# A three-stage attention and mixture-of-experts kernel: another engine repeats the block means of v in the first attention batch, and the search constants are made in five parts

## The chip, the cores and the metric

The kernel runs on one core of one Trainium2 chip. The metric is the device time of one execution in microseconds (us). The five engines of a core that appear below are TensorE (PE, with its weight loads PEld), VectorE (DVE), ScalarE (ACT), GpSimd (POOL) and SyncE (SP), which only issues DMAs here. Each engine works through its own list of instructions in order. An instruction whose data are not ready holds up everything behind it on its engine.

## The reference, cut to what matters

```python
# 1. attention: B=4, H=8, S=768, D=64; blocks of 32, window 16
k_sum = k.reshape(B, H, 24, 32, D).max(axis=3)
v_sum = v.reshape(B, H, 24, 32, D).mean(axis=3)          # the block means of v
scores = [window scores with |i-j| < 16, else -1e9]  ++  [q . k_sum / 8 + log 32]
a   = softmax(scores)
x   = a @ concat([v, v_sum])                              # -> [3072, 512]
# 2. MoE with capacity: each token goes to one of 8 experts, greedy by gate logit, 384 per expert
x[mask_e] = relu(x[mask_e] @ w1[e]) @ w2[e]
# 3. soft MoE: 32 slots, softmax over tokens (dispatch) and over slots (combine)
out = combine @ (relu((dispatch.T @ x) @ m2w1) @ m2w2)
```

Everything is computed in float32. Products that need it are made in split precision: a rounded high part and a low part, which is the difference between the value and its high part (`wh` and `wl` for w1, two halves of `x` for the tokens).

## The kernel before

**Attention.** The 32 (batch, head) pairs are worked in 16 units of two heads; unit n belongs to batch b = n // 4 and has p = n % 4. A batch's values lie in one tile, `vw[128, 12, 8, 65]`: for each of 12 tiles T of 64 queries and each head, partitions 0 to 95 hold the 96 rows of v that the window can touch, partitions 96 to 119 hold the 24 block means of v, and column 64 holds ones (so that the product also yields the softmax sum). The block means are the same for every T, so they have to stand there twelve times. There are two such tiles, used by turns.

A unit is software-pipelined over two turns of the main loop. Turn n does, in this order of code: the transposes of k for unit n+1 (`prep_k`, L199 and L214), the score products of unit n (`score`, L268), the minimum per row (`least`, L280 and L281 on DVE), the subtraction of the minimum (`less`, L285 on POOL), the key windows of unit n+1 (`windows`, L222 on POOL), the transposes of the exponentials of unit n-1 (`trans`, L295 and L297), exponentials (L289 on ACT), block maxima of k (L231 on DVE, spread by L236 on POOL), the transposes of q (`prep_q`), then the product with the values of unit n-1 (`av`, L306), its normalisation (`norm`, L320 to L322 on DVE) and the loads of unit n+4 (`load_qk`, L111). Each of the three groups of scores of a unit has its own `least`, `less` and exponential.

In the first batch the block means are made for two heads at a time, in the turn of the unit that owns these heads: `vsum` multiplies v by a summing matrix (L177), ACT copies the sums (L185), a second small product moves them to partitions 96 to 119 (L188), ACT writes them to tile T = 0 (L189), and a DMA issued by SP copies tile 0 to tiles 1 to 11 (L190). In the later batches one `vsum` makes all eight heads, one unit ahead.

All five engines follow the order of the code (a manual schedule). SP's list therefore has the copies of L190 among the loads of k, q and v (L111, L79, L91); `load_qk(4)` and the whole of the second batch's v are issued in turn 0.

**The search constants.** The expert assignment is searched in rounds on DVE with small tables (`_assign_consts`, L464 and after): counting tables, powers, selection matrices, a triangular mask, index rows. They are made once, at the end of turn 2: some 25 small DVE instructions, the index rows by POOL (`iota`), together with the load of `phi` and its selection matrix `selr`.

**The first MoE stage** starts after the attention with products of w2 and `phi` on PE, between which the search runs (DVE tables `D_r`, `G_r`, `tie_r` and small PE products `as`). Then the tokens of the first expert are gathered (L1154 on POOL), transposed (L1169), and split into high and low parts (L1170 on ACT, L1177 on DVE). The weights of w1 come in pieces of 128 columns; `split` makes their high part on ACT (L1199) and their low part on POOL (L1200). Two pieces are split ahead of the first matmuls of L1233, the third at their start.

Of the kernel before, what the change touches and what calls it, by code (L numbers as in the profile page):

```python
# [10 lines left out]
F32 = mybir.dt.float32  # L11
# [3 lines left out]
I32 = mybir.dt.int32  # L15
# [32 lines left out]
def _attention(tc, K, ps, q, k, v, w_gate, w2, xd, L, constants, work):  # L48
# [4 lines left out]
    with ExitStack() as ctx:  # L53
# [116 lines left out]
        def vsum(b, lo, hi, pv2s):  # L170

            vw = vws[b % 2]
            n = 64 * (hi - lo)
            pv = bank([128, n], f"pv{b}_{lo}")
            for T in range(NT):
                g = T % 4
                nc.tensor.matmul(  # L177
                    pv[32 * g : 32 * g + 32, :],
                    bz[0:96, 30 - 2 * T : 62 - 2 * T],
                    vw[0:96, T, lo:hi, 0:64],  # L180
                    start=T < 4,
                    stop=T >= NT - 4,
                )
            vs = wk.tile([128, 512], F32, name=f"vs{b}_{lo}", tag="vs", bufs=1)[:, 0:n]
            nc.scalar.copy(vs, pv)  # L185
            yield
            pv2 = bank([128, n], f"pw{b}_{lo}")
            nc.tensor.matmul(pv2[96:128, :], sel, vs, start=True, stop=True)  # L188
            nc.scalar.copy(vw[96:120, 0, lo:hi, 0:64], pv2[96:120].rearrange("j (h d)->j h d", d=64))  # L189
            nc.sync.dma_start(  # L190
                vw[96:120, 1:NT, lo:hi, :], vw[96:120, 0:1, lo:hi, :].to_broadcast([24, NT - 1, hi - lo, 65])
            )

        def turned(n, src, nm_, dst, put):
# [178 lines left out]
        prep_q(0)  # L373

        VS = {}
        for n in range(NU):
            b, p = divmod(n, 4)
            if 0 < n and n + 1 < NU:
                prep_k(n + 1)
            score(n)  # L380
            if n == 0:
                prep_k(1)
            if b == 0:
                VS[p] = vsum(0, 2 * p, 2 * p + 2, None)
                next(VS[p])
            least(n, 0)
            less(n, 0)
            if n + 1 < NU:
                windows(n + 1)
            if n:  # L390
                for i in range(3):
                    trans(n - 1, i)
            exps(n, 0)
            least(n, 1)
            less(n, 1)
            if n + 1 < NU:
                summaries(n + 1)
                if p == 3 and b:
                    gate_sum(b - 1, 0)
                    gate_sum(b - 1, 1)  # L400
                prep_q(n + 1)
            if p == 2 and b:
                gate_logits(b - 1, 0)
                gate_logits(b - 1, 1)
            if b == 0:
                next(VS[p], None)
            elif p == 0:
                next(VS[b, 0], None)
            exps(n, 1)
            least(n, 2)  # L410
            if n + 1 < NU:
                summaries_out(n + 1)
            less(n, 2)
            if n:
                av(n - 1)
                norm(n - 1, 0)
                norm(n - 1, 1)
            load_qk(n + 4)
            if n > 1:
                for i in range(2):  # L420
                    gate_turn(n - 2, i)
            exps(n, 2)
            if p == 0 and b + 1 < B:
                load_ends(b + 1)
                load_v(b + 1, range(H))
            if p == 0 and b:
                store(b - 1)
            if p == 3 and b + 1 < B:
                VS[b + 1, 0] = vsum(b + 1, 0, H, None)
                next(VS[b + 1, 0])  # L430
            if n == 2:
                constants(wk)
            if n == NU - 3:
                next(work)
        n = NU - 1
# [25 lines left out]
        next(work)  # L461


def _assign_consts(tc, cp, wk, ident):  # L464
    nc = tc.nc
    C = {}
    tmp = wk.tile([128, 480], I32, name="as_tmp", tag="X", bufs=6)
    it = tmp[:, 0:64]
    nc.gpsimd.iota(it, pattern=[[1, 64]], base=0, channel_multiplier=0)
# [4 lines left out]
    for n in (32, 64):  # L474

        C["o", n] = cp.tile([128, 128], BF16, name=f"as_o{n}")
        nc.vector.memset(C["o", n], float(STEP * n // 128))
    w8i = tmp[:, 64:72]
    nc.gpsimd.iota(w8i, pattern=[[-1, 8]], base=8, channel_multiplier=0)
    C["w8"] = cp.tile([128, 8], F32, name="as_w8")  # L480
# [7 lines left out]
    nc.vector.tensor_copy(C["w23"][0:1], w8i[0:1])  # L488
    C["ones"] = cp.tile([128, 128], BF16, name="as_on")
    nc.vector.memset(C["ones"], 1.0)  # L490
    for n in (32, 64):

        J = 128 // n
        C["pick", n] = cp.tile([128, J, J, n], F16, name=f"as_pk{n}")
        for j in range(J):
            nc.vector.tensor_copy(C["pick", n][:, j], ident[:, None, j:128:J].to_broadcast([128, J, n]))
    C["tri"] = cp.tile([128, 128], BF16, name="as_tri")
    nc.vector.memset(C["tri"], 1.0)
    nc.gpsimd.affine_select(
# [21 lines left out]
    for i in range(2):  # L521
        R = cp.tile([128, 2, 26], F16, name=f"as_R{i}")
        nc.vector.tensor_scalar(R[:, :, 25:26], pi[:, None, :].to_broadcast([128, 2, 1]), 0.5, None, ALU.mult)
        C["R"].append(R)
    return C


def _assign_rounds(tc, C, wk, ps, L, ids, eis, found, placed):
# [372 lines left out]
def tile_kernel(  # L901
# [60 lines left out]
    eis = cp.tile([128, E], I32, name="eis")  # L962

    def constants(wk):
        K["C"] = _assign_consts(tc, pqp, wk, ident)
        phis = K["phis"] = pqp.tile([128, 4, NSLOT], F32, name="phis")
        nc.sync.dma_start(phis, phi.rearrange("(c p) s->p c s", p=128))

# [167 lines left out]
    with ExitStack() as c2:  # L1136
# [54 lines left out]
        def split(k):  # L1191

            fetch(k)
            while len(W) <= k and len(W) < len(RAW):
# [2 lines left out]
                wh = ring.tile([128, 4, 128], F32R, name=f"wh{r}_{u}", tag="wh", bufs=NWHL)  # L1197
                wl = ring.tile([128, 4, 128], F32R, name=f"wl{r}_{u}", tag="wl", bufs=NWHL)
                nc.scalar.copy(wh, raw)  # L1199
                nc.gpsimd.tensor_tensor(wl, raw, wh.bitcast(F32), ALU.subtract)  # L1200
                W[8 * r + u] = (wh, wl)

        def fetch_p(r):
# [537 lines left out]
```

## Time and profile before

| what | value |
|---|---|
| median of 3 runs | 593.9 us (591.81, 593.9, 593.99) |
| the profiled execution's own time | 592.53 us |
| its span in the trace | 590.8 us |
| busy: PE, DVE, ACT, POOL | 538.5, 344.0, 315.3, 216.1 us |
| mean granted clock of TensorE | 0.976 |

The profiled execution's time is 1.7 us longer than its span, and it lies within the three runs. PE is busy for 91% of the span. The first four fortieths of the span (59 us) are the exception: there PE is busy for 5, 7, 6 and 7 tenths, and from the fifth on for 8 or 9 tenths and more. The chain of waits that ends last is PE for 60%, DVE for 21%, ACT and DMA for 4% each.

In the rows below a time in us at the start of a row is its start from the beginning of the span. In rows of the timeline a bracket at the end says how long the engine stood idle before the row, and what released it.

### The profile page before, as it was taken

The page shows a single profiled execution, that of the slowest core. Times are in us where ns is not written, and L with a number is a line of the kernel's source. Part 1 is how long each engine was busy: PE and PEld are TensorE (multiplying, and loading weights), DVE is VectorE, ACT ScalarE, POOL GpSimd, SP SyncE. Part 2 cuts the span into 40 slices and gives each one's busy share as a digit, 9 for nine tenths or more (in the row PEclk, how much of TensorE's full clock was granted, in tenths as well). Part 3 has the DMA queues.
Part 4 walks back from the last instruction along what each step waited for, and adds up shares of the span by engine and source line. Part 5 has one row for each costly group of instructions (what it writes and reads, how often), then busy time and mean ns, then how long its engine had stood idle before and what let it go on. Part 6 is the DMA issues. An engine that isn't in the chain of part 4 may idle for free.

```text
span 590.8 us, 15076 instructions
## 1 busy us (share of the span) xinstructions
PE 538.5 (91%) x5765; PEld 393.4 (67%) x5765; DVE 344.0 (58%) x1113; ACT 315.3 (53%) x670; POOL 216.1 (37%) x262
## 2 busy tenths in 40 slices
PE   5767999999999999889999998999999999979994
PEld 3556677777787766477766676767677867753474
DVE  5655887887872766688777798855232213031342
ACT  2743787887865667354635536544664535321231
POOL 3531563544530000425244473445446463321000
PEclk9986999999999999899999999999999999998997
DMA  9996299698974897436358484674949896779997
GB/s 192 203 195 132 66 243 226 160 223 182 299 275 149 291 383 224 116 100 196 100 163 281 131 265 153 215 235 152 303 156 302 287 327 209 264 246 372 354 302 208
DMA packets 158898, 131.17 MB, mean 222 GB/s; under 512 B 43380, under 2 KB 130068, under 8 KB 158828
## 3 DMA queue, kind: packets, MB, share of 16 engines
q1 hardware_dynamic: 153020, 115.81, 68.9%
q0 software_dynamic: 4368, 13.37, 7.0%
q10 hardware_dynamic: 1440, 1.05, 0.6%
q8 instruction: 45, 0.74, 0.5%
q14 instruction: 25, 0.20, 0.1%
HBM read 113.98 MB, written 14.02 MB: 217 GB/s over the span
## 4 chain that ended last, share of the span: by engine, by line
PE 60%; DVE 21%; ACT 4%; DMA 4%; issue 3%; SPq 2%; POOL 2%; another core or an unknown queue 1%; POOLq 0%; DVEq 0%; ACTq 0%
PE ph L1233 15%; PE pwt L1032 4%; PE pp L997 3%; PE pS L268 3%; DMA w<-in_moe_w_dram 3%; PE po L306 3%; PE po L1692 3%; PE mh L1629 3%; DVE G_r L745 3%; PE pt L1254 2%; PE pS L1412 2%; PE l L1274 2%; PE pA L1307 2%; SPq L91 2%; PE pf L1651 2%
## 5 line engine op out<-in xcount | busy, mean ns | idle before, releaser
L1233 PE MATMUL ph<-x,wh 128*128 128x384 f32 x512 | 145.3, 359 | 0.0
L1200 POOL TENSOR_TENSOR wl<-raw,wh 128x512 fp32r<-128x512 f32 x64 | 85.1, 1333 | 132.0 <-ACT wh L1199 119.4
L1233 PEld LDWEIGHTS ph<-x,wh 128*128 128x128 f32 x512 | 88.4, 189 | 22.1 <-issue 19.4
L1233 PE MATMUL ph<-x,wl 128*128 128x384 f32 x256 | 88.4, 345 | 0.0
L285 POOL TENSOR_TENSOR X<-X,mn 128x480 f32<-128x480 f32 x48 | 47.3, 985 | 69.9 <-DVE mn L281 42.2
L1244 ACT ACTIVATE hT<-ph 128x384 f32<-128x384 f32 x64 | 31.2, 488 | 74.7 <-PE ph L1233 63.4
L1233 PEld LDWEIGHTS ph<-x,wl 128*128 128x128 f32 x256 | 48.1, 188 | 0.0
L1154 POOL DMA_INDIRECT xg<-xd,ids x24 | 23.3, 972 | 61.6 <-PE pwt L1032 52.4
L306 PE MATMUL po<-vw,AT 120*64 120x65 f32 x768 | 30.3, 235 | 13.3 <-DMA vw<-vw 13.3
L280 DVE TENSOR_TENSOR X<-pS,nm 128x480 f32<-128x480 f32 x48 | 31.4, 655 | 18.6 <-PE pS L268 17.9
L306 PEld LDWEIGHTS po<-vw,AT 120*64 120x64 f32 x768 | 27.3, 147 | 20.1 <-DMA vw<-vw 14.0
L1199 ACT CAST wh<-raw 128x512 fp32r<-128x512 f32 x64 | 39.9, 623 | 0.0
L1047 ACT COPY wt<-pwt 128x512 f32<-128x512 f32 x60 | 33.1, 590 | 11.8 <-PE pwt L1032 9.8
L214 ACT COPY kT<-pk 64x384 f32<-64x384 f32 x62 | 31.2, 503 | 12.1 <-PE pk L199 11.3
L1032 PE MATMUL pwt<-ident,pw 128*128 128x128 f32 x224 | 33.6, 281 | 1.1 <-ACT wt L1047 0.6
L1254 PE MATMUL pt<-ident,hT 128*128 128x128 f32 x192 | 33.9, 277 | 0.0
L281 DVE TENSOR_REDUCE mn<-X 128x4 f32<-128x480 f32 x48 | 31.4, 653 | 4.1
L268 PE MATMUL pS<-kwin,qT 64*64 64x120 f32 x768 | 32.1, 276 | 1.8 <-POOL kwin L236 1.8
L1256 ACT COPY h<-pt 128x384 f32<-128x384 f32 x64 | 30.2, 474 | 5.8 <-PE pt L1254 5.6
L289 ACT ACTIVATE X<-X 128x480 f32<-128x480 f32 x48 | 29.3, 610 | 6.5 <-POOL X L285 5.9
L268 PEld LDWEIGHTS pS<-kwin,qT 64*64 64x64 f32 x768 | 28.1, 138 | 5.2 <-POOL kwin L236 2.4
L1290 POOL DMA_INDIRECT cd<-ce,ids x24 | 24.5, 1020 | 17.6 <-DVE den L1404 13.7
(291 smaller groups left out, 1066.0 us busy)
## 6 DMA issues: line engine op xcount, KB each, us to landing
mw<-in_moe_w_dram SPq DMA_DIRECT2D x55, 512.0 KB
raw<-in_moe_w_dram SPq DMA_DIRECT2D x64, 256.0 KB
w<-in_moe_w_dram SPq DMA_DIRECT2D x30, 512.0 KB
pw<-in_moe_w_dram SPq DMA_DIRECT2D x28, 512.0 KB
vw<-in_v_dram SPq DMA_DIRECT2D x32, 240.0 KB
kt<-in_k_dram SPq DMA_DIRECT2D x32, 192.0 KB
qt<-in_q_dram SPq DMA_DIRECT2D x32, 192.0 KB
xd<-xb POOLq DMA_DIRECT2D x4, 1536.0 KB
```

Source lines behind the costliest of these rows:

```text
L214: lambda r, d, s: nc.scalar.copy(d, s) if n or r else nc.vector.tensor_copy(d, s),
L268: nc.tensor.matmul(PS[n][i][64 * u : 64 * u + 64, j, :], qT[r, 64 * T : 64 * T + 64], kwin[r, T, :], start=True, stop=True,)
L280: nc.vector.tensor_tensor(X, PS[n][i], nm[:, i // 2], ALU.add)
L281: nc.vector.tensor_reduce(mn, X, AX.X, ALU.min)
L285: nc.gpsimd.tensor_tensor(X, X, MN.pop((n, i))[:, :, None].to_broadcast([128, 4, 120]), ALU.subtract)
L306: nc.tensor.matmul(PO[n][T // 6][64 * (T % 2) : 64 * (T % 2) + 64, T // 2 % 3, hh, :], AT[n, i][0:120, j, 64 * u : 64 * u + 64], vw[0:120, ...
L1032: nc.tensor.transpose(pt[:, dc], PW[e, q][t][:, 128 * dc : 128 * dc + 128], ident)
L1047: nc.scalar.copy(wt[:, :, 128 * t : 128 * t + 128], pt)
L1199: nc.scalar.copy(wh, raw)
L1200: nc.gpsimd.tensor_tensor(wl, raw, wh.bitcast(F32), ALU.subtract)
L1233: nc.tensor.matmul(ph, a[:, dc], b[:, dc], start=dc == n == 0, stop=(dc, n) == (3, 2),)
L1254: nc.tensor.transpose(pt[:, c], HT[r, fc][:, 128 * c : 128 * c + 128], ident)
```

## The change

Three edits:

1. In the first batch only, POOL repeats the block means: L190's DMA is replaced by a `tensor_copy` of tile 0 to tiles 1 to 11 (64 columns; the ones in column 64 are set once at the start anyway). It stands in the code behind the third `less` of the unit, and so behind it in POOL's list. Later batches keep the DMA.
2. `_assign_consts` becomes a generator in four parts, and `phi` with `selr` is the fifth. One part is made at the end of each of the turns 0 to 4, where before all came at the end of turn 2. The index rows on POOL go with their parts.
3. The low parts of the first two pieces of w1 (first expert) are made on DVE. All others stay on POOL.

The core of the diff:

```diff
@@ vsum
-            nc.sync.dma_start(
-                vw[96:120, 1:NT, lo:hi, :], vw[96:120, 0:1, lo:hi, :].to_broadcast([24, NT - 1, hi - lo, 65])
+            if b:
+                nc.sync.dma_start(
+                    vw[96:120, 1:NT, lo:hi, :], vw[96:120, 0:1, lo:hi, :].to_broadcast([24, NT - 1, hi - lo, 65])
+                )
+                return
+            yield
+            nc.gpsimd.tensor_copy(
+                vw[96:120, 1:NT, lo:hi, 0:64],
+                vw[96:120, 0:1, lo:hi, 0:64].to_broadcast([24, NT - 1, hi - lo, 64]),
             )
@@ main loop of the attention
+        steps = constants(wk)
         for n in range(NU):
...
             if b == 0:
-                next(VS[p], None)
+                next(VS[p])
...
             less(n, 2)
+            if b == 0:
+                next(VS[p], None)
...
-            if n == 2:
-                constants(wk)
+            if n < 5:
+                next(steps, None)
@@ _assign_consts: a yield behind as_o, behind as_on, behind as_pk and at the end
@@ split
-                nc.gpsimd.tensor_tensor(wl, raw, wh.bitcast(F32), ALU.subtract)
+
+                (nc.gpsimd if r or u > 1 else nc.vector).tensor_tensor(wl, raw, wh.bitcast(F32), ALU.subtract)
```

**POOL at the end of turn 0.** X0_2 is the third group of scores of unit 0, X1_0 the first of unit 1, vw0 the values of the first batch, as_tmp the index row for the first part of the constants. Before:

```order
L285 TENSOR_TENSOR X0_2_290<-X0_2_290,mn0_2_291 128x480
L285 TENSOR_TENSOR X1_0_367<-X1_0_367,mn1_0_368 128x480
L222 COPY kwin0_93<-kT0_95 128x12x96
L285 TENSOR_TENSOR X1_1_395<-X1_1_395,mn1_1_396 128x480
L236 COPY kwin0_93<-ks2_400 128x12x24
```

Now:

```order
L292 TENSOR_TENSOR X0_2_289<-X0_2_289,mn0_2_290 128x480
L196 COPY vw0_97<-vw0_97 24x11x2x64
L479 IOTA as_tmp_313 128x64
L292 TENSOR_TENSOR X1_0_377<-X1_0_377,mn1_0_378 128x480
L229 COPY kwin0_93<-kT0_95 128x12x96
```

The copy of the block means and the index row stand between the last subtraction of one unit and the first of the next.

**DVE at the same place.** Before:

```order
L280 TENSOR_TENSOR X0_2_290<-pS0_2_207,nm_149 128x480
L281 TENSOR_REDUCE mn0_2_291<-X0_2_290 128x4
L280 TENSOR_TENSOR X1_0_367<-pS1_0_325,nm_149 128x480
L281 TENSOR_REDUCE mn1_0_368<-X1_0_367 128x4
L280 TENSOR_TENSOR X1_1_395<-pS1_1_326,nm_149 128x480
```

Now:

```order
L287 TENSOR_TENSOR X0_2_289<-pS0_2_207,nm_149 128x480
L288 TENSOR_REDUCE mn0_2_290<-X0_2_289 128x4
L483 CAST as_cn32_315<-as_tmp_313 128x128
L483 CAST as_cn64_317<-as_tmp_313 128x128
L487 MEMSET as_o32_319 128x128
L487 MEMSET as_o64_321 128x128
L287 TENSOR_TENSOR X1_0_377<-pS1_0_335,nm_149 128x480
```

The first part of the constants stands ahead of the minimum of unit 1, and its first instruction reads POOL's index row. The second part does the same at the end of turn 1.

**SP in turn 0.** vw1 is the tile of the second batch, kt5 and qt5 are the loads of unit 5. Before:

```order
L162 DMA wg_167<-in_moe_w_gate_dram 128x4x8
L190 DMA vw0_97<-vw0_97 24x11x130
L111 DMA kt4_296<-in_k_dram 128x3x128 x2
L111 DMA qt4_299<-in_q_dram 128x3x128 x2
L79 DMA vw1_98<-in_v_dram 80x8x64 x2
L91 DMA vw1_98<-in_v_dram 96x10x64 x8
L190 DMA vw0_97<-vw0_97 24x11x130
L111 DMA kt5_460<-in_k_dram 128x3x128 x2
```

Now:

```order
L162 DMA wg_167<-in_moe_w_gate_dram 128x4x8
L111 DMA kt4_296<-in_k_dram 128x3x128 x2
L111 DMA qt4_299<-in_q_dram 128x3x128 x2
L79 DMA vw1_98<-in_v_dram 80x8x64 x2
L91 DMA vw1_98<-in_v_dram 96x10x64 x8
L111 DMA kt5_470<-in_k_dram 128x3x128 x2
```

The copies are gone, the order of the loads is the same.

**DVE ahead of the first expert.** M_b is a step of the search, x the low part of the first expert's tokens. Now (before, the rows of wl0 were not there and stood on POOL right ahead of that of the third piece):

```order
L767 TENSOR_SCALAR D1_r2_4071<-D_r20_4067 128x24
L894 TENSOR_TENSOR KM_b1_3647<-KM_b1_3647,KM_b0_3139 128x24
L558 TENSOR_REDUCE M_b2_4074<-L2_s2_4053 128x24
L1218 TENSOR_TENSOR wl0_0_4086<-raw0_0_3880,wh0_0_4085 128x512
L1218 TENSOR_TENSOR wl0_1_4090<-raw0_1_3891,wh0_1_4089 128x512
L1194 TENSOR_TENSOR x_3023<-px0_0_4097,x_3023 128x384
L1194 TENSOR_TENSOR x_3023<-px0_1_4108,x_3023 128x384
```

The two subtractions stand between the search and the tokens' low parts. The order of PE and of ACT is unchanged throughout.

## Rows read from the trace of the kernel before

**Rows 1.** Busy time by stretch; columns: stretch, PE, PEld, DVE, ACT, POOL, clock, DMA
```profile
40.00:60.00 20.00, 11.37 (x168) 9.91 (x170) 9.19 (x42) 6.74 (x15) 3.89 (x10) 0.74 0.76 137
```
**Rows 2.** Timeline of PE, first batch; columns: start, us, engine, line, operation, idle before
```profile
27.14 0.33 PE L306 MATMUL po<-vw,AT 120*64 120x65 f32 x2
29.74 2.63 PE L306 MATMUL po<-vw,AT 120*64 120x65 f32 x46 [2.27 <-DMA vw<-vw]
...
48.39 2.86 PE L306 MATMUL po<-vw,AT 120*64 120x65 f32 x46 [9.16 <-DMA vw<-vw]
...
59.47 1.67 PE L306 MATMUL po<-vw,AT 120*64 120x65 f32 x48
...
65.86 1.87 PE L268 MATMUL pS<-kwin,qT 64*64 64x120 f32 x48
```
**Rows 3.** Timeline of SP's queue: the second batch's v and the copy behind it
```profile
30.45 11.61 SPq L91 DMA_DIRECT2D vw<-in_v_dram  x8
42.16 1.14 SPq L190 DMA_DIRECT2D vw<-vw  x1
```
**Rows 4.** Groups of POOL up to 100 us, by form; columns: busy us, mean ns, idle
```profile
L285 POOL TENSOR_TENSOR X<-X,mn 128x480 f32<-128x480 f32 x24 | 23.7, 986 | 35.4 <-DVE mn L281 18.1 <-DVE rc L320 6.6 <-PE pA L295 4.5
L222 POOL COPY kwin<-kT 128x1152 f32<-128x1152 f32 x8 | 9.1, 1143 | 3.8 <-ACT kT L214 2.6 <-issue 1.2
L236 POOL COPY kwin<-ks 128x288 f32<-128x288 f32 x9 | 3.8, 421 | 0.6 <-DVE ks L231 0.6
...
L118 POOL MEMSET vw<- 32x512 f32 x2 | 1.0, 516 | 0.0
```
**Rows 5.** Timeline of POOL: the third subtraction of unit 0, an index row
```profile
21.20 0.99 POOL L285 TENSOR_TENSOR X<-X,mn 128x480 f32<-128x480 f32 x1 [0.90 <-DVE mn L281]
...
41.90 0.19 POOL L469 IOTA as_tmp<- 128x64 int32 x1
```
**Rows 6.** Timeline of DVE: start of unit 1, the constants, unit 3, start of unit 4
```profile
21.44 0.66 DVE L280 TENSOR_TENSOR X<-pS,nm 128x480 f32<-128x480 f32 x1 [0.32 <-PE pS L268]
...
52.19 0.35 DVE L473 CAST as_cn<-as_tmp 128x128 bf16<-128x128 int32 x2
...
53.29 0.97 DVE L496 CAST as_pk<-ident 128x128 f16<-128x128 f32 x6
54.24 0.17 DVE L498 MEMSET as_tri<- 128x128 bf16 x1
...
56.07 0.39 DVE L970 TENSOR_REDUCE selr<-ident 128x32 f32<-128x128 f32 x1
...
56.98 0.65 DVE L280 TENSOR_TENSOR X<-pS,nm 128x480 f32<-128x480 f32 x1
...
62.19 0.65 DVE L281 TENSOR_REDUCE mn<-X 128x4 f32<-128x480 f32 x1
...
64.06 0.56 DVE L322 TENSOR_TENSOR xb<-po,rc 128x384 f32<-128x384 f32 x1
66.95 0.66 DVE L280 TENSOR_TENSOR X<-pS,nm 128x480 f32<-128x480 f32 x1 [2.33 <-PE pS L268]
```
**Rows 7.** Timeline of ACT: k of unit 2, third exponential of unit 1
```profile
22.86 2.08 ACT L214 COPY kT<-pk 64x384 f32<-64x384 f32 x4
...
30.05 0.60 ACT L289 ACTIVATE X<-X 128x480 f32<-128x480 f32 x1 [0.82 <-POOL X L285]
```
**Rows 8.** Waits of PE from 110 to 250 us: total, times, longest
```profile
PE as L776 <- DVE G_r L745: 2.3, 1, 2.3
```
**Rows 9.** Timeline of POOL ahead of the first expert
```profile
239.28 3.73 POOL L1200 TENSOR_TENSOR wl<-raw,wh 128x512 fp32r<-128x512 f32 x3
```
**Rows 10.** Timeline of DVE at the same place
```profile
239.97 3.09 DVE L849 TENSOR_SCALAR tie_r<-tie_r,as 128x24 f32<-128x24 f32 x1 [1.23 <-PE pwt L1032]
...
249.49 0.25 DVE L804 SCALAR_TENSOR_TENSOR D_r<-D_r,as,E_r 128x24 bf16<-128x24 f32 x1 [1.50 <-PE as L801]
```
**Rows 11.** All instructions of L849: min/median/max ns, first and last start
```profile
L849 DVE TENSOR_SCALAR tie_r<-tie_r,as x7: 230/235/3092, 214.9 to 413.2; 128x24 f32<-128x24 f32 x7
```

More of the change, by code (lines that the diff above doesn't have):

```diff
@@ L461, in _attention, with _assign_consts @@
         next(work)
-def _assign_consts(tc, cp, wk, ident):
+def _assign_consts(tc, C, cp, wk, ident):
     nc = tc.nc
-    C = {}
     tmp = wk.tile([128, 480], I32, name="as_tmp", tag="X", bufs=6)
@@ L477, in _assign_consts @@
         nc.vector.memset(C["o", n], float(STEP * n // 128))
+    yield
+    tmp = wk.tile([128, 480], I32, name="as_tmp2", tag="X", bufs=6)
     w8i = tmp[:, 64:72]
@@ L490, in _assign_consts @@
     nc.vector.memset(C["ones"], 1.0)
+    yield
     for n in (32, 64):
@@ L496, in _assign_consts @@
             nc.vector.tensor_copy(C["pick", n][:, j], ident[:, None, j:128:J].to_broadcast([128, J, n]))
+    yield
+    tmp = wk.tile([128, 480], I32, name="as_tmp3", tag="X", bufs=6)
     C["tri"] = cp.tile([128, 128], BF16, name="as_tri")
@@ L524, in _assign_consts @@
         C["R"].append(R)
-    return C
+    yield
 def _assign_rounds(tc, C, wk, ps, L, ids, eis, found, placed):
@@ L964, in constants @@
     def constants(wk):
-        K["C"] = _assign_consts(tc, pqp, wk, ident)
+        C = K["C"] = {}
+        for _ in _assign_consts(tc, C, pqp, wk, ident):
+            yield
         phis = K["phis"] = pqp.tile([128, 4, NSLOT], F32, name="phis")
```

## Prediction

> **What bounds the kernel now.** I read the page first: PE is busy nine tenths of the time everywhere but in the first 60 us, so what is to be won without removing PE work lies there. The view by stretches says how much: from 40 to 60 us PE is busy for 11.37 us of 20, at a granted clock of 0.74 [rows 1]. The timeline of PE then names the holes. In turn 1 the products with v start, stop after two matmuls and go on when the copied block means arrive, 2.27 us later; in turn 2 the same takes 9.16 us [rows 2]. SP's queue says why the second is so long: the copy stands behind eight loads of the next batch's v, is issued at 42.16 and has arrived at 48.39, 6.2 us after [rows 3, 2]. Behind each hole PE runs slower for a while: 46 of these matmuls take 2.63 and 2.86 us, and 48 take 1.67 us later [rows 2]. DVE shows a second delay behind that hole: the constants stand between 52.19 and 56.98, and unit 3's minima only follow them [rows 6].
>
> **Edit 1, and the part of edit 2 that stands in its way.** With the DMA gone, the block means come from POOL one turn before PE wants them. What paces the first units then is a loop through DVE, POOL and ACT. I follow it with stretches that the trace shows.
>
> Lengths: the DVE work of a unit from its first X to the end of its third mn is 56.98 to 62.84, 5.86 us without a hole, its normalisation runs to 64.62, 1.8 us more [rows 6]. A subtraction on POOL is 0.99 [rows 5], an exponential 0.60 [rows 7]. From the start of the copies of k on ACT to the products with v on PE it is 22.86 to 27.14, 4.28 us [rows 7, 2]. The new copy has 11 x 2 x 64 = 1408 elements per partition. POOL copies 1152 in 1.143 us and 288 in 0.421, so 0.84 ns for each further element: 1.143 + 256 x 0.84 ns = 1.36 us [rows 4]. Only 24 partitions take part; 512 elements on 32 partitions in 0.516 us show no penalty for that [rows 4]. Bounds: 0.42, the 288-element row, and the rate of the two-input subtraction, 986 ns for 480, which gives 2.9 us [rows 4]. I take 1.36, from the two rows of the same operation.
>
> The Trainium skill (GPSIMD Engine Reference, section 3.1 on elementwise work) puts the best case at about 1.8 cycles per element, 512 elements in 768 ns: by that page 1408 elements are an estimated 2.1 us, and the forecast below would be 1.6 us later. The trace's 1152 elements in 1.143 us are faster than that rule, so the rows decide.
>
> Turn 0: POOL's third subtraction ends at 22.19 [rows 5], the copy at 23.55, the index row (0.19 [rows 5]) at 23.74. DVE meanwhile stands before its first constant, since that reads the index row. Parts one and two of the constants took 52.19 to 53.29 together [rows 6]; I give each half, 0.55. Unit 1's first X starts at 24.3 instead of 21.44 [rows 6], 2.9 us later. The cover for this is that PE and ACT still work on unit 0, so av of unit 0 keeps its 27.14, now without the stop.
>
> Turn 1: third mn of unit 1 at 24.3 + 5.86 = 30.15; subtraction, 31.15; exponential, 31.8; then ACT copies k. Av of unit 1 at 31.8 + 4.28 = 36.1, where before it went on at 48.39. POOL: copy to 32.5, index row to 32.7. DVE has normalised unit 0 by 32.0 and waits again for the index row; part two, and X of unit 2 at 33.25.
>
> Turn 2: mn at 33.25 + 5.86 = 39.1, subtraction 40.1, exponential 40.7, av of unit 2 at 45.0, against 59.47 [rows 2]: 14.5 us earlier. From there PE has no hole to speak of up to the scores of unit 4: before, 59.47 to 65.86 [rows 2]. So these come at 51.4, also 14.5 us earlier, provided DVE is there: it ends unit 2 at 39.1 + 1.8, makes part three (53.29 to 54.24, 0.95 [rows 6]) by 41.85, unit 3's third mn by 47.7 and its normalisation by 49.5. Part four waits for POOL (subtraction 48.7, copy 50.05) and took 54.24 to 56.07 [rows 6], so it ends near 51.9. Unit 4's first X came 1.09 us after the scores began (66.95 to 65.86 [rows 6, 2]), that is now 52.5: hidden, with 0.6 us to spare. Without the two waits for index rows the loop would be 2.5 us faster; that price is in the 14.5. The clock's loss goes too, as no hole of PE in this account exceeds 1 us; it is part of the difference read from PE's starts and is not added.
>
> The loads: v of the second batch is wanted near 47.5, and was all issued by 42.06 [rows 3], now 1 us sooner; with the copy's 6.2 us as delay it has arrived by 47.3. This is the tightest place of the account, and I charge nothing.
>
> **Rest of edit 2.** Part five (selr, 56.07 to 56.98, 0.9 us [rows 6]) falls into turn 4, where PE is busy and DVE is some tenths short of it: between 0 and 0.9, I take 0.4 lost.
>
> **Edit 3.** At 239.28 POOL makes three low parts in a row, 3.73 us [rows 9]. A DVE instruction that normally takes 0.235 us [rows 11] starts at 239.97, and ends when they do, at 243.06 [rows 10]: it was held by POOL. The search then reaches PE late, which waits 2.3 us, its longest wait between 110 and 250 us [rows 8]. With one low part left there, it ends at 239.28 + 1.24 = 240.5, and DVE's instruction 2.4 us earlier; PE's 2.3 us go. The two on DVE cost about 0.7 each (480 elements are 0.65 [rows 6]), 1.4, ahead of the tokens' low parts. DVE waits there for PE (1.50 us [rows 10]), so most of it is hidden. Bounds: +2.3 if all is hidden, -1.4 if the hold stays and nothing is. I take +2.0.
>
> **Sum.** 14.5 - 0.4 + 2.0 = 16.1 us off the profiled execution's 592.5: 576.4. The runs' median is 1.4 above that execution, which would make 577.8; I forecast **577**. PE is dense behind 60 us, and the loads hang on its progress, so all later work moves up with it.
>
> **Rivals.**
> - *POOL's copy is long and DVE waits for it.* A copy of c us enters the loop in turns 0 and 1, and beyond 0.6 us more in turn 3. At 2.9 us: 2 x 1.53 + 0.9 = 4.0 us later, 581. For it: the 24 partitions and the repeated source are in no row. Against: the two copy rows. Chance 0.15.
> - *The loads become the bound of the first batch.* If the queue needs some 3 to 6 us more than PE's new pace, v of the second batch or k of unit 5 is what PE waits for: 580 to 583. For it: the margin of 0.2 us. Against: PE waited for no other load there, and less is in the queue. Chance 0.10.
> - *The index rows cost DVE less than I charge*, because the copy is shorter or DVE catches up: up to 2.5 us better, 574. Chance 0.08.
> - *The change does not do what it says:* if the products of unit n-1 waited for the copy of unit n, not of n-1, PE would stand still again from 27.5 to 32.5, and each turn would grow from 9 to some 11.7 us: 585. Against: before, the products of unit 0 went on at 29.74, long before the second copy was issued. Chance 0.02.
> - *Slower than before.* The same POOL copy, if it were several times its price, would be worse than the DMA: beyond 1.36 us each microsecond counts in turns 0, 1, 3 and, beyond 1.65 us more, in turn 2. The loss is 4 x (c - 1.36) - 2.25 us; it eats the 16.1 us at c = 6.0, and at 7 us the time is 597. Nothing in the rows is near that. Chance 0.03, other mishaps included.
>
> **How the numbers follow.** The forecast has 0.62, with 574 to 580 as its own range. The range of 8 in 10 takes in the larger copy and most of the loads' rival: 572.5 to 583. About 0.5% is what a measurement of this kernel can tell from no change, 3 us. Faster by more than that is everything but the last rival and a sliver: 0.95; within it 0.02; slower 0.03.
>
> **What would show it.** Right: no wait of PE for vw in turns 1 and 2; four POOL copies of 24 partitions near 1.36 us; DVE idle for POOL's index row for some 2.5 us ahead of as_cn and under 1 us ahead of the second part; scores of unit 4 near 51.4; tie_r at about 0.6 us and PE's wait for G_r gone. Wrong: copies of 3 us and more, PE waiting for loads of v, k or q before 60 us, a clock below 1 between 30 and 60 us, or a hole of PE at the low parts on DVE; or a saving at unit 4 that is gone again at the end.

## The result, and the profile after

The changed kernel took 577.14 us (median of 4 runs, 575.30 to 580.23) where the kernel before took 593.16 in runs on the same chip (4 runs, 591.81 to 593.99): a ratio of 0.972, with a 95% interval of 0.968 to 0.976. Run again on another chip it was 572.57 against 589.84, 0.970 (0.967 to 0.973). The profiled execution took 575.3 us, with a span of 573.6.

The stretches that answer to [rows 1], with the same columns, are now filled, at the full clock:

```profile
20.00:40.00 20.00, 17.20 (x309) 13.82 (x311) 15.53 (x39) 15.35 (x31) 12.44 (x16) 1.00 1.20 195
40.00:60.00 20.00, 19.36 (x304) 14.05 (x296) 17.93 (x47) 16.24 (x32) 13.19 (x18) 1.00 0.75 164
```

PE's timeline, against [rows 2] (start, us, engine, line, operation). The products with v of units 0, 1 and 2 run in one piece, in 1.67 us each, and the scores of unit 4 start at 51.84, 14.0 us earlier than before:

```profile
27.07 1.67 PE L313 MATMUL po<-vw,AT 120*64 120x65 f32 x48
...
36.31 1.67 PE L313 MATMUL po<-vw,AT 120*64 120x65 f32 x48
...
45.92 1.67 PE L313 MATMUL po<-vw,AT 120*64 120x65 f32 x48
...
51.84 1.87 PE L275 MATMUL pS<-kwin,qT 64*64 64x120 f32 x48
```

From 20 to 250 us PE's waits for the copies of the block means fall from 13.3 us in five waits to 2.0 us in three, those of the later batches, which keep the DMA.

POOL's timeline: the new copies of units 0 to 2 (the fourth, at 49.98, is like them), and the first index row behind one of them:

```profile
22.20 1.36 POOL L196 COPY vw<-vw 24x1408 f32<-24x1408 f32 x1
23.64 0.19 POOL L479 IOTA as_tmp<- 128x64 int32 x1
...
31.42 1.36 POOL L196 COPY vw<-vw 24x1408 f32<-24x1408 f32 x1
...
40.66 1.36 POOL L196 COPY vw<-vw 24x1408 f32<-24x1408 f32 x1
```

DVE's timeline, against [rows 6]: parts one to four of the constants, each behind POOL. Three wait for an index row (the bracket is the idle time before, and what ended it). The picks of part three, as_pk, stand in no bracket, but take 1.91 us instead of 0.97: they start while POOL's copy of 40.66 runs. (The picks are the selection matrices of the search.)

```profile
23.86 0.36 DVE L483 CAST as_cn<-as_tmp 128x128 bf16<-128x128 int32 x2 [2.79 <-POOL as_tmp L479]
24.42 0.59 DVE L287 TENSOR_TENSOR X<-pS,nm 128x480 f32<-128x480 f32 x1
...
33.02 0.17 DVE L493 CAST as_w<-as_tmp 128x8 f32<-128x8 int32 x1 [1.02 <-POOL as_tmp L491]
...
41.16 1.91 DVE L509 CAST as_pk<-ident 128x128 f16<-128x128 f32 x6
...
52.15 0.36 DVE L520 CAST as_sf<-as_si 128x384 f16<-128x384 int32 x1 [1.38 <-POOL as_si L518]
...
53.01 0.65 DVE L287 TENSOR_TENSOR X<-pS,nm 128x480 f32<-128x480 f32 x1
```

The later units stay 14.0 us early up to the scores of unit 11 (115.09 against 129.13). Between these and unit 12's, 0.8 us are lost, all of it in the block sums of the fourth batch's v: 24 matmuls take 3.69 us here and took 2.87 before, at full clock in both. The timeline of their weight loads (PEld) has a wait for a DMA after the second, which before has none. The sums read only v and a constant, so the DMA that they need is a load of v, although the trace names one of q that ended with it.

```profile
122.95 0.14 PEld L177 LDWEIGHTS pv<-vw,bz 96*32 96x32 f32 x2 [0.17 <-issue]
123.84 0.19 PEld L177 LDWEIGHTS pv<-vw,bz 96*32 96x32 f32 x8 [0.75 <-DMA qt<-in_q_dram]
```

At the first gather POOL is 13.2 us early (222.40 against 235.61). Then edit 3 acts. POOL's timeline there, against [rows 9], one low part in place of three; the fourth comes 17.1 us early (before: 256.36), so 3.9 us were won between:

```profile
222.40 1.06 POOL L1171 DMA_INDIRECT xg<-xd,ids  x1 [52.45 <-PE pwt L1049]
...
226.08 1.28 POOL L1218 TENSOR_TENSOR wl<-raw,wh 128x512 fp32r<-128x512 f32 x1
239.25 1.28 POOL L1218 TENSOR_TENSOR wl<-raw,wh 128x512 fp32r<-128x512 f32 x1 [11.90 <-DVE G_r L760]
```

DVE there, against [rows 10], and PE's products of w2 and phi (pp): tie_r ends with POOL's one low part, PE no longer waits for G_r, and the two groups of pp take 1.49 and 1.50 us, where before they took 2.46 and 2.08.

```profile
226.75 0.65 DVE L864 TENSOR_SCALAR tie_r<-tie_r,as 128x24 f32<-128x24 f32 x1 [1.23 <-PE pwt L1049]
...
233.90 1.28 DVE L1218 TENSOR_TENSOR wl<-raw,wh 128x512 fp32r<-128x512 f32 x2
```
```profile
229.12 1.49 PE L1014 MATMUL pp<-wt,phis 128*32 128x256 f32 x20
230.54 0.20 PE L803 MATMUL as<-c_r,as_pk 128*128 128x8 f16 x2
230.68 1.50 PE L1014 MATMUL pp<-wt,phis 128*32 128x256 f32 x22
```

At the end of the program 17.2 us of span are left: what was won at these two places reaches the end.

### The profile page after: what moved, and what is told of

Its sections match the earlier page's. It is cut to its first block, busy times and chain, and to the rows that moved or that the text cites. A ratio compares the mean times of both kernels' runs of the same rounds, so it can differ in the third digit from the quotient of the medians.

```text
span 573.6 us, 15062 instructions
## 1 busy us (share of the span) xinstructions
PE 531.9 (93%) x5765; PEld 387.8 (68%) x5765; DVE 342.4 (60%) x1115; ACT 315.9 (55%) x670; POOL 219.0 (38%) x264
## 3 DMA queue, kind: packets, MB, share of 16 engines
HBM read 113.98 MB, written 14.02 MB: 223 GB/s over the span
## 4 chain that ended last, share of the span: by engine, by line
PE 61%; DVE 19%; DMA 6%; ACT 5%; issue 4%; POOL 3%; another core or an unknown queue 1%; SPq 0%; POOLq 0%; DVEq 0%; ACTq 0%
PE ph L1251 15%; DMA w<-in_moe_w_dram 5%; PE pwt L1049 4%; PE pp L1014 3%; PE po L1710 3%; PE pS L275 3%; PE po L313 3%; PE mh L1647 2%; PE pS L1430 2%; PE pt L1272 2%; DVE G_r L760 2%; PE l L1292 2%; PE pA L1325 2%; PE pf L1669 2%; PE pv L177 2%
## 5 line engine op out<-in xcount | busy, mean ns | idle before, releaser
L1218 POOL TENSOR_TENSOR wl<-raw,wh 128x512 fp32r<-128x512 f32 x62 | 82.6, 1334 | 132.7 <-ACT wh L1216 104.4
L313 PEld LDWEIGHTS po<-vw,AT 120*64 120x64 f32 x768 | 24.9, 137 | 8.6 <-issue 3.1
L760 DVE TENSOR_TENSOR G_r<-D_r,as_cn 128x768 bf16<-128x768 bf16 (+1 forms) x41 | 29.2, 713 | 1.2
```

The costliest lines, as they stand in the source:

```text
L313: nc.tensor.matmul(PO[n][T // 6][64 * (T % 2) : 64 * (T % 2) + 64, T // 2 % 3, hh, :], AT[n, i][0:120, j, 64 * u : 64 * u + 64], vw[0:120, ...
L760: v.tensor_tensor(G, Dg.rearrange("p (q j)->p q j", j=J)[:, :, None, :].to_broadcast([128, 24 // J, n, J]), C["cn", n][:, None].to_broadca ...
L1218: (nc.gpsimd if r or u > 1 else nc.vector).tensor_tensor(wl, raw, wh.bitcast(F32), ALU.subtract)
```

## The experiments

Kernels in one of the three groups below ran on one chip and share the runs of the kernel before.

### Each edit alone, and another queue (before: 589.72 us)

**e1_copy_only**: edit 1 alone; the constants stay in one piece in turn 2, as before. The edit in short:

```
+            yield
+            nc.gpsimd.tensor_copy(
+                vw[96:120, 1:NT, lo:hi, 0:64],
+                vw[96:120, 0:1, lo:hi, 0:64].to_broadcast([24, NT - 1, hi - lo, 64]),
+            )
```

> Edit 1 alone: POOL repeats the block means, the constants stay in one piece at the end of turn 2, the low parts stay on POOL. Theory: the DMA's place in SP's queue was the loss, and parts one and two of the constants cost the changed kernel some 2 us because DVE waits for index rows behind the copy. Then without the parts unit 1's first X is back near 21.4, the products with v of units 0 and 1 start without a wait near 27.1 and 35, and the scores of unit 4 start near 49 to 50, 2 us earlier than with edits 1 and 2 (51.84); the block of constants (4.8 us on DVE) is then partly visible in turn 3. Search and first expert as before (2.3 us wait of PE). Time about 577 to 579. Rival: the constants in one piece cost their 4.8 us in full, as they did before, and the parts are what made the gain possible; then the scores of unit 4 start at 54 or later and the time is above 581.

Measured: 581.13 us, ratio 0.986 (0.982 to 0.991). The rival was right. The products with v of unit 2 start at 43.27, 2.65 us earlier than in the kernel after, since no index row holds the first two turns; but then the undivided constants with selr stand on DVE from 39.22 until X of unit 3 follows at 43.99. PE's timeline shows what comes of it: a wait of 3.58 us, after which the six transposes of x (px) take 1.54 us (0.88 in the kernel after) and the block sums 5.14 (2.79 as a rule), and unit 4's scores come at 55.87.

```profile
43.27 1.67 PE L313 MATMUL po<-vw,AT 120*64 120x65 f32 x48
48.52 1.54 PE L349 MATMUL px<-ident,xb 128*128 128x128 f32 x6 [3.58 <-ACT vw L189]
49.99 5.14 PE L177 MATMUL pv<-vw,bz 96*32 96x512 f32 x24
...
55.87 1.87 PE L275 MATMUL pS<-kwin,qT 64*64 64x120 f32 x48
```

**e2_parts_only**: edit 2 alone; the copies stay DMAs. In the main loop:

```
-            if n == 2:
-                constants(wk)
+            if n < 5:
+                next(steps, None)
```

> Edit 2 alone: the constants in five parts, the DMA and POOL's low parts as before. Theory: the 9.2 us wait for the second copy stays (SP's order is that of before but for phi), the parts one and two vanish behind it, and only the minima of unit 3 come earlier (56.98 before, near 55 now, bounded by the scores at 53.9). Scores of unit 4 near 64, time 590 to 592, 1 to 3 us under before. Rival: the parts are worth the whole 4.8 us of the block, 588 or less.

Measured: 589.23 us, ratio 0.998 (0.996 to 1.001). PE still waits for the second copy, now for 11.40 us, and the scores of unit 4 come at 64.63, 1.2 us earlier than before. So the parts by themselves are worth about 1 us: the constants were mostly beside a hole that was there anyway.

```profile
47.66 2.86 PE L306 MATMUL po<-vw,AT 120*64 120x65 f32 x46 [11.40 <-DMA vw<-vw]
```

**e3_low_only**: edit 3 alone.

```
-                nc.gpsimd.tensor_tensor(wl, raw, wh.bitcast(F32), ALU.subtract)
+                (nc.gpsimd if r or u > 1 else nc.vector).tensor_tensor(wl, raw, wh.bitcast(F32), ALU.subtract)
```

> Edit 3 alone: two low parts on DVE. Theory: tie_r falls from 3.09 to 0.65 us, PE's wait for G_r of 2.3 us is gone, and the products of w2 and phi behind it no longer run at the lower clock, which is worth 1.5 us more; together 3.9 us between the gather of the first expert and its third low part, time near 589.5. Rival: the 3.9 us of the changed kernel come from its other alignment of search and PE; alone the edit is worth the 2.3 us of the wait less 1.3 us of DVE work, about 1 us, 592 to 593.

Measured: 585.37 us, ratio 0.994 (0.991 to 0.997). From the gather (233.67) to the fourth low part (250.52) it is 16.85 us, as in the kernel after, and 20.75 before: 3.9 us, as the theory said, with the wait for G_r gone.

**e4_act_queue**: the kernel before, with the first batch's copies issued by ACT instead of SP.

```
-            nc.sync.dma_start(
+            (nc.sync if b else nc.scalar).dma_start(
```

> The kernel before, with the first batch's copies still made by DMA but issued by ACT, right behind its own write of tile 0, not by SP. Theory: it was the place in SP's list that made the copy late; issued at 20 and 28.7 it arrives within some 6 us, before 27 and 35, so PE has no wait for it and the scores of unit 4 start at 49 to 50; time 577 to 579, like edit 1 alone. Rival: the 16 DMA engines are full with loads until 54 us, so a copy of 134 KB in small pieces is late whoever issues it; then waits of several us for the block means stay and the time is 583 or more.

Measured: 602.63 us, ratio 1.024 (1.021 to 1.027), slower. ACT's timeline (ACTq is its sequencer) shows why. ACT stood until it could issue the copy, with the exponentials behind it. In the program each DMA of SP and ACT waits for an earlier one with which it shares a counter, and the second hold ended with a load of k. So another queue didn't free the copy of the loads; it made ACT wait for them too. This run can't say what the place in SP's queue alone is worth; e9 below can.

```profile
33.72 1.41 ACTq L190 DMA_DIRECT2D vw<-vw  x1
35.18 1.10 ACT L289 ACTIVATE X<-X 128x480 f32<-128x480 f32 x2 [15.52 <-issue]
...
51.09 1.09 ACT L289 ACTIVATE X<-X 128x480 f32<-128x480 f32 x2 [8.25 <-DMA kt<-in_k_dram]
```

Alone, the edits give 8.6, 0.5 and 4.4 us, 13.4 in sum; together 17.3 (after_again, below), on a chip where the kernel before takes the same time. The 3.8 us more belong to edits 1 and 2: both together, without edit 3, give 13.8 us (e12_no_low, below), where one by one they give 9.1; edit 3 gives 0.9 us less beside them than alone. At unit 4's scores edits 1 and 2 give 14.0 us together and 10.0 and 1.2 alone, so 2.8 us of it show in the first batch; the rest is not traced to a place.

### The terms of the account (before: 594.62 us)

**e5_double**: the kernel after, with each POOL copy made twice.

```
-            nc.gpsimd.tensor_copy(
+            for _ in range(2):
+                nc.gpsimd.tensor_copy(
```

> The kernel after, with each unit's GpSimd copy of the block means made twice in a row (1.36 us more on GpSimd in each of the four turns). My step: the copy is not hidden behind GpSimd's other work, since the first subtraction of the next unit (and in turns 1 and 3 the next index row) stands behind it; so each doubling costs nearly its whole 1.36 us in three of the turns and the scores of unit 4 come 3 to 4.5 us later (near 55.5). Rival: GpSimd has slack in a unit turn, the copy costs nothing, and the scores of unit 4 stay within 1 us of 51.84.

Measured: 583.75 us, ratio 0.979 (0.973 to 0.985). The scores of units 2, 3, 4 and 5 come 1.38, 2.96, 2.84 and 3.79 us later than in the kernel after. So another 1.36 us of POOL cost 1.4 and 1.6 us in the turns 0 and 1, nothing in turn 2 and 1.0 in turn 3: the theory's three turns, 2.84 us at unit 4 where it gave 3 to 4.5, the last part a unit later. In turn 2 no index row stands behind the copy, and in the kernel after POOL is idle for 2.47 us before its next subtraction (44.49); the second copy fits in there, although the copies and the picks held each other and the pair takes 3.67 us here and 2.8 in the other turns.

```profile
43.62 3.67 POOL L197 COPY vw<-vw 24x1408 f32<-24x1408 f32 x2
```

**e6_rows_early**: the kernel after, with all index rows made by POOL ahead of the unit loop, in a tile of their own. The edit in short:

```
-    tmp = wk.tile([128, 480], I32, name="as_tmp", tag="X", bufs=6)
+    tmp = wk.tile([128, 1024], I32, name="as_tmp", tag="mw")
...
+    nc.gpsimd.iota(w8i, pattern=[[-1, 8]], base=8, channel_multiplier=0)
+    nc.gpsimd.iota(si, pattern=[[1, CAP]], base=0, channel_multiplier=0)
...
+    yield
...
-        for _ in _assign_consts(tc, C, pqp, wk, ident):
+        for _ in _assign_consts(tc, C, pqp, pre0, ident):
```

> The kernel after, with all index rows of the search constants made by GpSimd ahead of the unit loop (in a tile of their own), so that the VectorE parts of the constants no longer stand behind a GpSimd subtraction or copy. My step: in the kernel after, VectorE loses 2.8 us at as_cn (23.86), 1.0 at as_w (33.02) and 1.4 at as_sf (52.15), and I put 2.5 us of the first four units down to these waits. Expected: scores of unit 4 near 49 to 49.5 instead of 51.84, each av(1), av(2) 2 to 2.5 us earlier, the gather likewise, ratio to before near 0.968 (after: 0.972), that is 2 to 2.5 us faster than the kernel after. Rival: GpSimd's third subtraction is what the next X waits for in any case, then the waits only change their name and the scores of unit 4 stay at 51.5 to 52.

Measured: 574.88 us, ratio 0.965 (0.961 to 0.970). DVE's idle times ahead of the constants are gone and X of unit 1 starts at 21.23 instead of 24.42. But only 1.4 us of that arrive at unit 4's scores (50.40), so the theory's 2 to 2.5 was too much. DVE's timeline shows the limit: the third X of unit 1 stands behind q of unit 2, which waits for PE, and PE is still at unit 0's work. A part of the waits also came back as a hold: the first cast of part two (as_w) now starts while POOL's copy of 29.77 runs and takes 0.83 us, where it takes 0.17 in the kernel after.

```profile
26.12 1.15 DVE L257 TENSOR_SCALAR qT<-pq 64x384 f32<-64x384 f32 x2 [0.52 <-PE pq L206]
27.30 0.66 DVE L287 TENSOR_TENSOR X<-pS,nm 128x480 f32<-128x480 f32 x1
```

**e8_low_twice**: the kernel after, but POOL makes the first two low parts again and VectorE repeats them.

```
-                (nc.gpsimd if r or u > 1 else nc.vector).tensor_tensor(wl, raw, wh.bitcast(F32), ALU.subtract)
+                nc.gpsimd.tensor_tensor(wl, raw, wh.bitcast(F32), ALU.subtract)
+                if not r and u < 2:
+                    nc.vector.tensor_tensor(wl, raw, wh.bitcast(F32), ALU.subtract)
```

> The kernel after, but GpSimd makes the first two w1 low parts too, as before, and VectorE repeats them at the place where it makes them now: the work moved onto VectorE stays, the work taken from GpSimd comes back. Theory: the gain of this edit is GpSimd's alone, through tie_r's hold and the TensorE wait of 2.3 us behind it, with a clock loss of about 1.5 us after that wait; so tie_r takes about 3 us again, the wait for G_r is back, and the stretch from the gather to the fourth low part is about 20.7 us instead of 16.85 (a kernel about 3.9 us slower than after; ratio to before near 0.978). Rival: the gain is an earlier low part, not GpSimd's relief; then the stretch stays near 17.

Measured: 577.73 us, ratio 0.971 (0.966 to 0.976). tie_r takes 3.07 us again and PE waits 2.3 us for G_r, so the gain is POOL's relief and not an earlier low part. But the stretch from the gather to the fourth low part is 19.22 us, 2.4 more than after and not 3.9: the clock stays at 1.00 behind the wait. The time alone does not tell this kernel from the one after, which had 0.972 on another chip; e12 below was therefore run beside it.

**e9_loads_later**: the kernel before, with the loads of the second batch's v issued at the end of turn 1, behind the second copy.

```
-            if p == 0 and b + 1 < B:
+            if p == (b == 0) and b + 1 < B:
                 load_ends(b + 1)
                 load_v(b + 1, range(H))
```

> The kernel before, with the loads of the second batch's v (ten DMA issues) taken out of turn 0 and issued at the end of turn 1, behind the second copy of the block means; the copies stay DMAs on SyncE's queue. If the place in the queue makes the waits of 2.3 and 9.2 us (second copy issued at 42.16 behind eight loads that take 11.6 us to issue), the 9.2 us wait is gone, the second copy is issued by about 32, and the scores of unit 4 come 7 to 10 us earlier than 65.86, near the 55.87 of the kernel with the GpSimd copy alone: ratio near 0.987. Rival: the copy itself is slow as a DMA, whatever stands ahead of it (wait over 4 us at av(1) remains), or the loads only move the hold to the third copy (then po of unit 2 waits instead, and the scores of unit 4 come no earlier than 62).

Measured: 587.66 us, ratio 0.988 (0.981 to 0.995). Each side was half right. The 9.16 us of [rows 2] are gone: the second copy is issued at 29.07 and unit 1's products run at 37.00 without a stop. (The 2.3 us for the first copy, which stands ahead of the loads in both kernels, stay.) But the eight loads now stand ahead of the third copy, issued at 46.00, and unit 2's products wait 5.64 us for it; unit 4's scores come at 59.24, 6.6 us earlier than before. SP's queue and PE show it:

```profile
34.81 11.09 SPq L91 DMA_DIRECT2D vw<-in_v_dram  x8
46.00 1.02 SPq L190 DMA_DIRECT2D vw<-vw  x1
```
```profile
37.00 1.67 PE L306 MATMUL po<-vw,AT 120*64 120x65 f32 x48
...
51.72 2.86 PE L306 MATMUL po<-vw,AT 120*64 120x65 f32 x46 [5.64 <-DMA vw<-vw]
...
59.24 1.87 PE L268 MATMUL pS<-kwin,qT 64*64 64x120 f32 x48
```

So the hold goes with the place behind the eight loads; a copy on POOL has no such place. The place is not all of it: this wait begins at 46.1, when the third copy has just been issued, and lasts until it has landed, 5.7 us after its issue.

### The kernel after beside three of its relatives (before: 589.84 us)

**after_again** is the kernel after, unchanged.

> The kernel after, unchanged, beside the three others on one chip, so that they can be set against it directly. Expected: ratio to before 0.970 to 0.975.

Measured: 572.57 us (571.88 to 573.21), ratio 0.970 (0.967 to 0.973).

**e12_no_low**: the kernel after with edit 3 undone.

```
-                (nc.gpsimd if r or u > 1 else nc.vector).tensor_tensor(wl, raw, wh.bitcast(F32), ALU.subtract)
+                nc.gpsimd.tensor_tensor(wl, raw, wh.bitcast(F32), ALU.subtract)
```

> The kernel after with its third edit undone (all w1 low parts on GpSimd), on the same chip as the kernel after. Theory: tie_r takes about 3.1 us, TensorE waits 2.3 us for G_r, and the clock may fall after that wait (it did in four of the five profiles with that wait, costing about 1.5 us); so the stretch from the gather to the fourth low part is 19.2 to 20.75 us instead of 16.85 and the time 2.4 to 3.9 us longer than the kernel after. Rival: what follows takes it back, and the two differ by less than 1 us.

Measured: 576.06 us (574.30 to 578.68), ratio 0.977 (0.974 to 0.980): 3.5 us more than the kernel after, and no run of the one reaches into the runs of the other. In the profiled execution the stretch from the gather to the fourth low part is 19.17 us, 2.3 more than 16.85, again without a fall of the clock; this execution was the quickest of the six. DVE and POOL there: tie_r ends with the third low part.

```profile
225.54 4.09 DVE L864 TENSOR_SCALAR tie_r<-tie_r,as 128x24 f32<-128x24 f32 x1 [0.22 <-PE as L701]
```
```profile
225.86 3.72 POOL L1218 TENSOR_TENSOR wl<-raw,wh 128x512 fp32r<-128x512 f32 x3
```

**e6_again** is the kernel with the early index rows.

> The kernel after with all index rows of the constants made by GpSimd ahead of the unit loop, on the same chip as the kernel after. Its first profile had unit 4's scores at 50.40 (after: 51.84) and the gather at 220.82 (222.40), 1.4 to 1.6 us earlier. Theory: these 1.5 us last to the end, so 1 to 2 us faster than the kernel after. Rival: the end of the kernel takes them back (its first profiled span was only 1.1 us shorter), and the two differ by less than 0.5 us.

Measured: 570.81 us (569.05 to 574.82), ratio 0.968 (0.965 to 0.972). Unit 4's scores come at 50.82 against 52.09 in after_again, 1.3 us earlier, the fourth low part 1.0 us earlier, and the median is 1.8 us lower; but one of its six runs is above all five of the kernel after. The profiles show the 1.3 us at its place twice; for the whole program the gain is likely and not settled.

**e10_rows_third**: early index rows, and the third low part on VectorE too. Beside the edit of e6:

```
-                (nc.gpsimd if r or u > 1 else nc.vector).tensor_tensor(wl, raw, wh.bitcast(F32), ALU.subtract)
+                (nc.gpsimd if r or u > 2 else nc.vector).tensor_tensor(wl, raw, wh.bitcast(F32), ALU.subtract)
```

> The kernel with the early index rows, and the third w1 low part on VectorE too, so that GpSimd makes none in the search's tie stage. By the step on the low parts (the hold on tie_r is what cost), tie_r falls from 0.65 to about 0.2 us. Theory: nothing on TensorE waits for tie_r any more in the kernel after, so the 0.45 us is hidden, and VectorE's block of low parts (1.28 us for two) grows by 0.6 us in front of c_r, for which TensorE waits: no gain, up to 0.6 us slower than the kernel with early rows. Rival: the hold still sets TensorE's pace, and the kernel is 0.4 us or more faster.

Measured: 572.75 us (570.75 to 575.21), ratio 0.970 (0.967 to 0.973). As the theory said: tie_r falls to 0.30 us, VectorE's low parts take 1.89 us instead of 1.28, and from the gather to the fourth low part it is 17.46 us instead of 16.85. Nothing is won by freeing the last of POOL. Against its own base, e6_again, the median is 1.9 us higher, more than the theory's 0.6, but the runs of the two overlap.

```profile
225.02 0.30 DVE L864 TENSOR_SCALAR tie_r<-tie_r,as 128x24 f32<-128x24 f32 x1 [0.22 <-PE as L701]
...
233.18 1.89 DVE L1218 TENSOR_TENSOR wl<-raw,wh 128x512 fp32r<-128x512 f32 x3
```

Ahead of unit 12's scores, this kernel's block sums wait 1.25 us for the DMA for which the kernel after waits 0.75.

## Why the prediction was right, step by step

| step | forecast | measured |
|---|---|---|
| POOL's copy | 1.36 us | 1.36, four times |
| X of unit 1, behind POOL's index row | 24.3 | 24.42 |
| products with v of unit 1 | 36.1 | 36.31 |
| products with v of unit 2 | 45.0 | 45.92 |
| scores of unit 4 | 51.4, 14.5 us earlier | 51.84, 14.0 us earlier |
| part five of the constants | -0.4 us | 0: units 5 to 11 stay 14.0 early |
| loads of later v | not charged | -0.8 us, at unit 12 |
| edit 3 | +2.0 us | +3.9 us |
| sum | 16.1 us | 17.1 us, 17.2 at the end |
| profiled execution | 576.4 | 575.3 |
| median | 577 | 577.14 |

**The copy.** The two POOL rows of the same operation gave its length to the hundredth; 24 partitions and a repeated source cost nothing extra. The 2.1 us that the prediction worked out from the Trainium skill (GPSIMD Engine Reference, section 3.1) are not what this trace has. e5 bears out that it isn't hidden: a second copy cost 1.4 and 1.6 us in turns 0 and 1.

**The hole.** That the second copy's place behind eight loads made the long wait is shown by e9, where the wait moves to the copy that then stands behind them. e2 and e3 show that neither of the other edits takes it away by itself (PE waits 11.40 and 9.91 us there), and e1 that without the parts its removal is worth 10.0 us at unit 4, not 14.0. The prediction followed DVE through both edits in one account, which is why it came near.

**Unit 2's products, 0.9 us late.** Two terms of the loop were short, by about half of it each. ACT's copies of k in turn 3 start at 41.13, where the account has 40.7, since X of unit 2 was 0.4 us late already (33.65 for 33.25). From there to the products it takes 4.79 us, where the account carried over unit 0's 4.28 (unit 1's took 4.29); here ACT stands idle for 0.32 us ahead of its second copy of the transposed exponentials (AT), and the copies of k take 2.22 us instead of 2.08 [rows 7].

```profile
41.13 2.22 ACT L221 COPY kT<-pk 64x384 f32<-64x384 f32 x4
44.45 1.07 ACT L304 COPY AT<-pA 120x512 f32<-120x512 f32 x2 [0.32 <-ACT AT L304]
```

Half of the 0.9 us was made good by unit 4's scores.

**The picks.** Another step of the account failed in size, "makes part three (53.29 to 54.24, 0.95 [rows 6]) by 41.85": the picks took 1.91 us and ended at 43.07, since POOL's copy ran when they started. Unit 2's products do not stand behind them, but unit 3's first X does (42.99), and behind that part four and unit 4's first X. This came 1.17 us after the scores began, against 1.09 before, so the 0.6 us to spare were used up and PE lost next to nothing. That two engines' instructions can hold each other I had used for tie_r and not for this pair. The Trainium skill (SBUF — State Buffer, "Who interferes with whom") says that a cast or tensor_scalar of VectorE in its two-port mode and a GpSimd instruction exclude each other, and that the first to issue keeps the other out until it ends; the trace agrees for the picks, of which the first takes 1.06 us and ends at 42.22, just behind the copy that ends at 42.02. For tie_r it agrees in part: in e12 its row begins 0.32 us ahead of POOL's first subtraction, and it is held all the same until the third ends. Which of the two was issued first the rows do not show.

**The index rows** were priced at 2.5 us within the 14.5. e6 takes their waits away and gains 1.4 us at unit 4: the loop would have met PE, still busy with unit 0, and POOL's copy, which holds the first cast of part two; I had looked for neither. The rival that the index rows cost DVE less than charged was therefore a small one.

**Part five** costs nothing. Unit 5's scores are 14.02 us early, as unit 4's; the 0.9 us of selr fit in turn 4.

**The loads.** The rival "the loads become the bound" came true in a small way and in another place: not for the second batch, where I saw a margin of 0.2 us, but for the fourth, at 0.8 us. (The second batch's loads were not issued 1 us sooner, as the account had it: the eight stand in SP's queue from 31.39 to 42.19, and PE did not wait for them.) Why the fourth batch's v is late is not shown. PE's faster pace alone does not explain it: e8 begins these sums at 122.84, as early as the kernel after (122.95), and takes 3.08 us for them, while e4 and e9 come to them later (146.43 and 130.33) and take 3.59 and 3.70. That it is a load of v rests on what the instruction reads; no run was made that issues these loads earlier.

**Edit 3** was the mis-sized term: 2.0 forecast, 3.9 measured, alone (e3) and with the others. The mechanism was right: tie_r's time goes with the number of low parts that POOL makes beside it, 0.30 us with none, 0.65 and 1.66 with one, 3.04 to 4.11 with three, and it always ends with the last of them. PE's 2.3 us went as forecast, and VectorE's 1.28 us for two low parts cost nothing there, so all 2.3 were won. What the account lacked is what follows such a wait: in the kernel before, and in e1, e2 and e9, PE runs at the lower clock behind it, for more than 3 us. The groups of pp took 2.46 + 2.08 us before and 1.49 + 1.50 after: 1.55 us. The stretches of e1 and e12 at the same place, some 4.5 us after the wait began, show that the loss does not always come:

```profile
237.00:239.00 2.00, 2.00 (x22) 0.87 (x21) 0.63 (x4) 0.06 (x1) 0.00 (x0) 0.50 0.00 0
```
```profile
233.00:235.00 2.00, 2.00 (x26) 0.81 (x20) 1.07 (x6) 0.00 (x0) 0.00 (x0) 1.00 0.00 0
```

The first is e1, with the granted clock at 0.50 (1.2 GHz), the second e12, at 1.00 (2.4 GHz), both after the same wait of 2.3 us. Of the seven profiles with that wait, four show the fall and three (e4, e8, e12) do not; in e4 the two groups of pp take 1.49 and 1.50 us. What decides it stays open. So edit 3 is worth 2.3 us where the clock holds and 3.9 where it falls; in whole times it was 4.4 alone and 3.5 beside the others.

**The sum** was 1.0 us short, since the 1.9 us too little for edit 3 outweigh the 0.5 and 0.8 us too much at the other places less 0.4 for part five. The forecast then rounded 577.8 down, while the runs' median lay 1.8 us above the profiled execution where 1.4 was assumed; that these small errors meet at 577.1 is luck, that they are small is not.

## What to carry to other kernels

A small copy between two tiles of the same core belongs on an engine with room, if the queue that it would use carries long loads: what it cost here was its place behind them, and then 3.8 to 6.2 us from its issue until PE went on. Before its price is taken as hidden, look for what stands behind it on that engine; and when two edits take away the hole and the work that stood in its shade, price them together, since here 3.8 of 17.3 us came from no edit alone. Where a wait of TensorE goes, look at how fast it runs behind the wait: here that was worth two thirds of the wait again, in four profiles of seven.

## What the runs showed of the hardware that was not expected

- A VectorE instruction of 0.24 us [rows 11] stood for 4.09 us beside three GpSimd subtractions in a row (e12), until the last of them ended, although its row begins 0.32 us before the first. In e5 the hold went both ways: the picks held the second of two GpSimd copies, 2.24 us instead of 1.37.
- The clock fell to half behind a wait of 2.3 us in four profiles, and did not in three with the same wait in the same place.
- A DMA issue on ACT's queue kept ACT standing for 15.5 us, while SP's loads were under way.
